# Weights' words by one shift-and-or and a bfloat16-to-float16 copy, in half pieces; split products for chunk 0's feed-forward; a new order

## The chip, the cores and the metric

The kernel runs on one NeuronCore of a Trainium2 chip, in one launch. The metric is the device time of one execution in microseconds (us), as the median of several runs. The engines are PE (matrix products), DVE (vector), ACT (scalar), POOL (GpSimd) and SP, which here only issues transfers.

## The reference

A recurrent attention and then a feed-forward part with a maximum of three products in place of an activation. The weights `moe_w1`, `moe_w2`, `moe_w3`, `moe_w_out` arrive as 64-bit floats, all else as 32-bit floats.

```python
B, H, S, D = 4, 8, 768, 48          # batch, heads, steps, head width
for t in range(S):
    cur = einsum('bhd,bhe->bhde', u * k[t], v[t])
    y[t] = einsum('bhd,bhde->bhe', r[t], state + cur)
    state = w * state + einsum('bhd,bhe->bhde', k[t], v[t])
x = y, as 3072 rows of 384
h = maximum(maximum(x @ w1, x @ w2), x @ w3)      # 384 -> 768
out = h @ w_out                                   # 768 -> 384
```

## The kernel before

The 768 steps are cut into 12 chunks of 64 steps (`NCH`, `C`). The heads of a chunk are worked on in two halves, q = 0 and 1, of 8 units each. With the powers of `w` multiplied into `k` and `r` (`scale`), the attention of a chunk is: scores on PE, a mask on DVE with the `u` term on its diagonal (`product`, `total`, `diagonal`, `mask`), values on PE (from the masked scores and from the state before the chunk), and keys on PE, which bring the state forward (`into_state`). The result, transposed, is `x`: 256 tokens a chunk. The feed-forward of a chunk is 18 up products (6 blocks f of 128 columns, three weights i each, three matmuls of 128 x 256 a product) and a down part of 3 banks by 6 blocks. ACT copies the first product of a block to `m` (`first`), DVE folds in the other two (`least`).

From chunk 1 on, every factor is split into a high and a low part, and a product is three matmuls: high by high, low by high, high by low. In attention the parts are float16; in the feed-forward they are the float32r format (`xh`, `xl` for x; `hh`, `hl` for h; `wh`, `woh` and a low tile, `wlo` in the profile, for the weights). The left factors of attention's matmuls stand in tiles with gaps, `kb` (scores), `vb` (values), `ktb` (keys), `sb` (state), which transfers on SP fill from dense tiles `kd`, `vd`, `ktd`, `sd` (`spread`); the right ones are `rh`, `rl`, `ah`, `al`. Chunk 0 is different: attention (`full`, with `apart` filling the tiles on ACT) and feed-forward (the `else` branch of `mul`, and `part`) are done in plain float32 on the weights' words (`words`), so that the low parts need not be there yet.

The weights are 8 pieces of 1152 numbers on each partition, 6 for the up products and 2 for the down part. A piece comes as 64-bit words (`load_weight`, tile `raw64`). `convert` makes 32-bit words of them with three DVE instructions, lines 224 to 226, with the sign turned over (hence `ALU.min` in `least`); `round_up`, line 230, makes the high part on ACT; `leave`, line 234, subtracts it on DVE, after all pieces have been converted. Late in the kernel every piece is loaded again (`again`) to check on DVE and ACT that its exponents lie in the range that the conversion takes; if not, or if other checks fail, a slow general version behind a branch runs.

POOL (`helper`, `helping`) does scaling, products, diagonals and decay from chunk 2 on, and `hl` for blocks 0 to 4; before that DVE does them. The banks of PSUM are two pools of four: `psm` for the feed-forward, `psa` for attention. An up product takes the next `psm` bank as soon as its last reader is done.

The order of the instructions on each engine is written out by `Plan`. Each step is given an engine, a cost, a due time in chunks, what it reads, writes and takes from pools; `order` then plays the program through, taking on the engine that can start earliest the step with the lowest due time. A table `SHIFT` moves due times by kind of step, in chunks, with one number for the opening (due up to 1.6) and one for the rest. An argument `near` makes DVE steps dearer while POOL is busy. Each engine runs its list strictly in that order, and so does SP's list of transfers:

```python
t = min(when.values())
n = min((m for m in when if when[m] <= t + 0.02), key=lambda m: self.todo[m]["due"])
```

## Time and profile before

| what | value |
|---|---|
| runs | 424.49, 423.60, 424.29 us; median 424.29 |
| the profiled execution | 423.27 us, of which its span, first to last instruction, 421.5 us |
| TensorE clock granted | 1.000 |
| PE busy | 400.4 us (95% of the span) |
| DVE, ACT, POOL busy | 299.0, 245.4, 202.9 us |

The profile is one execution. Its page gives busy time by engine, the span in 40 slices of busy tenths, the chain of work that ended last, and the costliest groups of instructions. A group's row reads: line, engine, operation, output <- inputs, shapes, count, busy time, mean ns of one, and idle time before it with what ended it. PEld is the loading of weights into the array, which overlaps with PE's products. Tile names are cut short, so `raw` is `raw64`.

### The profile page before, as it was taken

Reading aid. Unit: us, or ns where it says so; the run is one execution under the profiler, and the core shown is the slowest. Engines: PE = TensorE matmul, PEld = TensorE weight load, DVE = VectorE, ACT = ScalarE, POOL = GpSimd, SP = SyncE. Lnnn points to the kernel's source line nnn. Section 1 sums busy time; section 2 is a strip of 40 time slices with the busy share of each in tenths; the row PEclk is TensorE's granted clock in tenths of the full one; section 3 lists DMA queues with packets and bytes.
Section 4 is the critical chain, followed back from the end, with each engine's and each line's share of the span. In section 5 each row is a group of like instructions: output and inputs, shape, how many; then the busy total and the mean of one; then the engine's idle time right before and its main releaser. Section 6 shows DMA issues by size and latency. Waiting matters only on the chain.

```text
span 421.5 us, 11698 instructions
## 1 busy us (share of the span) xinstructions
PE 400.4 (95%) x4686; PEld 390.7 (93%) x4686; DVE 299.0 (71%) x522; ACT 245.4 (58%) x612; POOL 202.9 (48%) x188
## 2 busy tenths in 40 slices
PE   2899999878999999999999999999999999999995
PEld 2898888868989999999999999999999999999995
DVE  6999999999998666765765765665665686354240
ACT  5798527454566656465466466366365478578241
POOL 8000008799679556555565555655564471011120
PEclk9999999999999999999999999999999999999999
DMA  8799897848889886965965975975875997856101
GB/s 297 303 330 287 252 273 236 239 104 264 262 213 274 227 222 167 286 177 136 277 185 144 273 188 146 271 186 147 265 189 154 262 343 210 261 191 226 39 2 45
DMA packets 28654, 90.12 MB, mean 214 GB/s; under 512 B 4528, under 2 KB 9392, under 8 KB 26544
## 3 DMA queue, kind: packets, MB, share of 16 engines
q1 hardware_dynamic: 23264, 84.47, 69.0%
q10 hardware_dynamic: 5328, 4.82, 3.6%
q8 instruction: 39, 0.64, 0.7%
q14 instruction: 23, 0.19, 0.2%
HBM read 45.85 MB, written 4.72 MB: 120 GB/s over the span
## 4 chain that ended last, share of the span: by engine, by line
PE 71%; DVE 11%; DMA 5%; issue 4%; ACT 4%; POOL 4%; SPq 0%; ACTq 0%; DVEq 0%; POOLq 0%
PE psm L463 59%; PE psa L385 11%; DVE wlo L225 2%; DMA out_dram<-io 1%; DMA ktb<-ktd 1%; DVE wlo L224 1%; DMA sb<-sd 1%; POOL hl L484 1%; DVE wlo L226 1%; DMA feat<-in_feat_dram 1%; PE psa L458 1%; DVE m L478 1%; POOL am L362 1%; POOL feat L342 1%; DVE wlo L234 1%
## 5 line engine op out<-in xcount | busy, mean ns | idle before, releaser
L463 PE MATMUL psm<-xh,wh 128*128 128x256 f32 x594 | 152.4, 287 | 2.3 <-DVE m L478 2.3
L463 PE MATMUL psm<-xl,wh 128*128 128x256 f32 x594 | 149.6, 282 | 0.0
L463 PEld LDWEIGHTS psm<-xh,wh 128*128 128x128 f32 x594 | 112.3, 189 | 3.3 <-DVE m L478 3.2
L463 PEld LDWEIGHTS psm<-xl,wh 128*128 128x128 f32 x594 | 112.3, 189 | 0.6 <-DVE xl L446 0.5
L463 PE MATMUL psm<-xh,wlo 128*128 128x256 f32 x594 | 103.0, 282 | 0.0
L478 DVE TENSOR_TENSOR m<-psm,m 128x256 f32<-128x256 f32 x138 | 57.8, 419 | 60.4 <-PE psm L463 45.4
L463 PEld LDWEIGHTS psm<-xh,wlo 128*128 128x128 f32 x594 | 85.3, 192 | 0.0
L342 POOL TENSOR_TENSOR feat<-feat,wrt 128x512 f32<-128x512 f32 x40 | 56.7, 1428 | 59.3 <-DMA feat<-in_feat_dram 59.2
L484 POOL TENSOR_TENSOR hl<-m,hh 128x256 fp32r<-128x256 f32 x55 | 47.1, 855 | 78.0 <-ACT hh L481 77.9
L481 ACT CAST hh<-m 128x256 fp32r<-128x256 f32 x66 | 26.8, 407 | 73.2 <-DVE m L478 72.9
L361 POOL TENSOR_TENSOR am<-tok,u_sb 128x384 f32<-128x384 f32 x20 | 24.4, 1222 | 57.9 <-DVE al L405 57.9
L463 PE MATMUL psm<-hh,woh 128*128 128x256 f32 x198 | 50.2, 286 | 0.0
L463 PE MATMUL psm<-hh,wlo 128*128 128x256 f32 x198 | 49.3, 281 | 0.0
L325 ACT ACTIVATE junk<-tok 128x384 bf16<-128x384 f32 x72 | 37.5, 521 | 7.5 <-DMA tok<-in_tok_dram 5.9
L463 PEld LDWEIGHTS psm<-hh,woh 128*128 128x128 f32 x198 | 37.5, 189 | 0.0
L463 PEld LDWEIGHTS psm<-hh,wlo 128*128 128x128 f32 x198 | 37.5, 189 | 0.0
L441 ACT ACTIVATE xh<-psa 32x256 fp32r<-32x256 f32 (+5 forms) x60 | 25.0, 417 | 19.1 <-PE psa L385 18.4
L446 DVE SCALAR_TENSOR_TENSOR xl<-psa,xh 32x256 fp32r<-32x256 f32 (+2 forms) x55 | 25.9, 470 | 13.9 <-ACT xh L441 13.0
L463 PE MATMUL psm<-hl,woh 128*128 128x256 f32 x198 | 32.6, 281 | 1.8 <-POOL hl L484 1.8
L314 DVE TENSOR_TENSOR kd<-feat,kd 128x512 f16<-128x512 f32 x22 | 21.3, 970 | 17.4 <-ACT kd L309 17.3
L385 PE MATMUL psa<-ah,vb 128*128 128x64 f16 x352 | 32.8, 194 | 0.0
L385 PE MATMUL psa<-al,vb 128*128 128x64 f16 x176 | 31.2, 193 | 1.4 <-DVE al L405 1.4
(102 smaller groups left out, 819.8 us busy)
## 6 DMA issues: line engine op xcount, KB each, us to landing
tok<-in_tok_dram SPq DMA_DIRECT2D x24, 576.0 KB, 6.6
raw<-in_ws_dram SPq DMA_DIRECT2D x12, 1152.0 KB, 8.2
feat<-in_feat_dram SPq DMA_DIRECT2D x24, 512.0 KB, 5.3
kb<-kd SPq DMA_DIRECT2D x22, 256.0 KB, 5.3
kb<-kd SPq DMA_DIRECT2D x22, 248.0 KB, 5.6
ktb<-ktd SPq DMA_DIRECT2D x20, 256.0 KB, 3.6
ktb<-ktd SPq DMA_DIRECT2D x20, 248.0 KB, 4.8
raw<-in_wo_dram SPq DMA_DIRECT2D x4, 1152.0 KB, 6.3
```

The source lines that it names most:

```text
L225: nc.vector.scalar_tensor_tensor(out=t, in0=rw[:, :, 0], scalar=29, in1=t, op0=ALU.logical_shift_right, op1=ALU.bitwise_or)
L314: nc.vector.tensor_tensor(out=dense.dense[:, 1, :, 0:w], in0=src, in1=dense.dense[:, 0, :, 0:w], op=ALU.subtract)
L325: nc.scalar.activation(out=junk, in_=src, func=AF.Square, scale=scale, accum_out=stat[:, kind, 2 * c + q:2 * c + q + 1])
L342: helper(c).tensor_tensor(out=t[n], in0=t[n], in1=tb, op=ALU.mult)
L361: helper(c).tensor_tensor(out=w.rearrange("p (g b) d -> p g b d", g=2), in0=t["r"], in1=by_token(u_sb, q), op=ALU.mult)
L385: nc.tensor.matmul(out=ps, lhsT=l[i], rhs=rr[j], start=first and n == 0, stop=last and n == 2)
L441: nc.scalar.mul(out=hi, in_=src, mul=SC_X)
L446: nc.vector.scalar_tensor_tensor(out=lo, in0=src, scalar=SC_X, in1=hi.bitcast(F32), op0=ALU.mult, op1=ALU.subtract)
L463: nc.tensor.matmul(out=ps, lhsT=a, rhs=b, start=first and n == 0, stop=last and n == len(prods) - 1)
L478: nc.vector.tensor_tensor(out=to, in0=ps, in1=m, op=ALU.min)
L481: nc.scalar.copy(out=h[0][:, f, :], in_=m)
L484: (nc.vector if f == NF - 1 else nc.gpsimd).tensor_tensor(out=h[1][:, f, :], in0=m, in1=h[0][:, f, :].bitcast(F32), op=ALU.subtract)
```

## The change

A weight's piece is loaded as two halves of 576 numbers (`HN`), as 16-bit words, at an offset of one 16-bit word in the tile, so that bits 16 to 47 of each number lie on a 32-bit word (`mids`). `tops`, on ACT, copies the top 16 bits of each number, read as bfloat16, into the upper halves of the words of a zeroed tile `ztop`, as float16; that turns the 11-bit exponent into an 8-bit one. `convert` is now one DVE instruction for a half, in place: shift the middle word right by 13, or the `ztop` word in. `round_up` and `leave` then work on each half at once, from `mids`. The sign is no longer turned, so `least` takes the maximum. The low parts have tiles of their own, `wl0` to `wl7`. `raw64` has four half buffers for two whole ones. The vetting works on halves of 32-bit words and a different test.

Chunk 0's feed-forward now uses the split products like the others, so chunk 0's x and h get low parts (`leave_x`; all of chunk 0's `hl` on DVE). `full` for the keys takes 112 of 128 columns. Chunk 2's scaling, products and decay move from POOL to DVE, its diagonals to ACT. The opening's column of `SHIFT`, the `near` rule and several costs are new; the other column is the same but for new and dropped kinds.

```diff
-        "act ah": (-2.85, -0.9), "act am": (-0.15, 0), "act hh": (-0.7, 0.4), ...
+        "act ah": (-5.31, -0.9), "act am": (2.08, 0), "act hh": (1.37, 0.4), ...
...
-                cost += self.NEAR * p["near"] * min(cost, free["pool"] - t)
+                cost += min(p["near"] * cost, p["near"] / (1 + p["near"]) * (free["pool"] - t))
...
-    wld = ctx.enter_context(tc.tile_pool(name="wld", bufs=2))
+    wld = ctx.enter_context(tc.tile_pool(name="wld", bufs=4))
...
-    wlo = ctx.enter_context(tc.tile_pool(name="wlo", bufs=NF + 3))
...
-    def convert(n, raw64, his):
-        rw = raw64.rearrange("p (n two) -> p n two", two=2)
-        t = wlo.tile([P, WN], I32, name="wlo")
-        words[n] = t.bitcast(F32)
-        nc.vector.tensor_scalar(out=t, in0=rw[:, :, 1], scalar1=0x0F000000, scalar2=3, op0=ALU.bitwise_xor, op1=ALU.logical_shift_left)
-        nc.vector.scalar_tensor_tensor(out=t, in0=rw[:, :, 0], scalar=29, in1=t, op0=ALU.logical_shift_right, op1=ALU.bitwise_or)
-        nc.vector.scalar_tensor_tensor(out=t, in0=rw[:, :, 1], scalar=-2 ** 27, in1=t, op0=ALU.bitwise_and, op1=ALU.bitwise_xor)
-        return his
-    def round_up(n, his):
-        nc.scalar.copy(out=his, in_=words[n])
-    def leave(n, his):
-        lows[n] = wlo.tile([P, WN], F32R, name="wlo")
-        nc.vector.tensor_tensor(out=lows[n], in0=words.pop(n), in1=his.bitcast(F32), op=ALU.subtract)
...
-        nc.scalar.activation(out=left, in_=left, func=AF.Abs, accum_out=odd[:, n:n + 1])
+    lows = [const.tile([P, WN], F32R, name=f"wl{n}") for n in range(NW)]
...
+    def load_weight(n, h, shift=0):
+        raw = wld.tile([P, 4 * HN + 4], I16, name="raw64")
+        src = (ws[n] if n < NF else wo[n - NF]).bitcast(I16)
+        nc.sync.dma_start(out=raw[:, shift:shift + 4 * HN], in_=src[:, h * 4 * HN:(h + 1) * 4 * HN])
+        return raw
+    ztop = [const.tile([P, HN], I32, name=f"ztop{h}") for h in range(2)]
+    for z in ztop:
+        nc.gpsimd.memset(z.bitcast(F32), 0.0)
+    def halves(raw, k):
+        return raw[:, 0:4 * HN].rearrange("p (n four) -> p n four", four=4)[:, :, k]
+    def mids(raw):
+        return raw.bitcast(I32)[:, 1:1 + 2 * HN].rearrange("p (n two) -> p n two", two=2)[:, :, 0]
+    def tops(h, raw):
+        nc.scalar.copy(out=ztop[h].bitcast(F16).rearrange("p (n two) -> p n two", two=2)[:, :, 1], in_=halves(raw[:, 1:], 3).bitcast(BF16))
+    def convert(h, raw):
+        nc.vector.scalar_tensor_tensor(out=mids(raw), in0=mids(raw), scalar=13, in1=ztop[h], op0=ALU.logical_shift_right, op1=ALU.bitwise_or)
+    def round_up(n, h, raw):
+        nc.scalar.copy(out=part_of(n, h)[0], in_=mids(raw).bitcast(F32))
+    def leave(n, h, raw):
+        hi, lo = part_of(n, h)
+        nc.vector.tensor_tensor(out=lo, in0=mids(raw).bitcast(F32), in1=hi.bitcast(F32), op=ALU.subtract)
...
+        nc.scalar.activation(out=t.bitcast(F32), in_=t, func=AF.Relu, bias=beyond, accum_out=odd[:, k:k + 1])
...
-        return nc.gpsimd if c > 1 else nc.vector
+        return nc.gpsimd if c > 2 else nc.vector
...
-        if c == 1:
+        if c in (1, 2):
...
-        nc.vector.tensor_tensor(out=to, in0=ps, in1=m, op=ALU.min)
+        nc.vector.tensor_tensor(out=to, in0=ps, in1=m, op=ALU.max)
...
+    def lows_by(c, f):
+        return nc.gpsimd if f < NF - 1 and c > 0 else nc.vector
...
+        dma(due, fetch, 8 * P * HN, takes=[("raw64", w)])
+        do(due - 0.05, "act", act(HN), lambda: tops(h, T[w]), reads=[w], writes=[("ztop", h)])
+        do(due, "dve", dve(HN), lambda: convert(h, T[w]), reads=[("ztop", h)], writes=[w], near=0.55)
+        do(due + 0.05, "act", act(HN), lambda: round_up(n, h, T[w]), reads=[w], writes=[("his", n, h)])
+        do(due + 0.1, "dve", dve(HN), lambda: leave(n, h, T[w]), reads=[w, ("his", n, h)], writes=[("lo", n, h)], near=0.6)
...
-        do(due, "pe", 3.65, lambda: full("ke", q, ktb, D, P, units(raws[c, q]["v"])), reads=["ktb", t], takes=[("psa", ("ke", c, q))])
+        do(due, "pe", 3.2, lambda: full("ke", q, ktb, D, C + D, units(raws[c, q]["v"])), reads=["ktb", t], takes=[("psa", ("ke", c, q))])
...
-                        for j in range(NJ):
-                            nc.tensor.matmul(out=ps, lhsT=by_up(words[f], i, j), rhs=T["x", 0][:, j, :], start=j == 0, stop=j == NJ - 1)
+                    T["up", c, f, i] = up(T["x", c], f, i, TOK)
```

How the order moves, engine by engine. First ACT, the last twelve rows up to its first copy of an up product to `m` (`junk` are sums of squares for the checks, `am` the diagonals, `sd` the state's high part). Before:

```order
L452 ACTIVATE ktb<-tok 64x8x48 x2
L325 ACTIVATE junk,stat<-tok 128x384
L373 ACTIVATE am<-cs,a 128x64 x8
L309 ACTIVATE kd<-feat 128x8x64
L441 ACTIVATE xh<-psa 96x256
L441 ACTIVATE xh<-psa 32x256 x3
L419 ACTIVATE state<-psa 128x192 x2
L325 ACTIVATE junk,stat<-tok 128x384
L230 CAST wh<-wlo 128x1152
L325 ACTIVATE junk,stat<-tok 128x384
L347 CAST rh<-feat 128x512
L474 COPY m<-psm 128x256
```

The same twelve rows up to that copy now; line 239 is `tops`, line 246 `round_up`:

```order
L239 CAST ztop_109<-raw_293 128x576
L349 ACTIVATE junk,stat<-tok 128x384 x3
L332 ACTIVATE vd_147<-tok 128x8x48
L239 CAST ztop_110<-raw_311 128x576
L443 ACTIVATE state<-psa 112x192 x2
L246 CAST wh<-raw_273 128x576
L349 ACTIVATE junk,stat<-state 128x384
L332 ACTIVATE kd<-feat 128x8x64
L246 CAST wh<-raw_293 128x576
L332 ACTIVATE sd<-state 128x8x48
L246 CAST wh<-raw_311 128x576
L498 COPY m<-psm 128x256 x2
```

The copy stood behind the third weight's rounding; now it stands behind four weights' tops and roundings, chunk 1's second diagonals not included, and behind both halves' state and `sd`.

Second DVE, from the second decay of chunk 0 on: the first weight (`raw_165`), before:

```order
L381 TENSOR_TENSOR tok<-tok,tkt 128x384
L224 TENSOR_SCALAR wlo<-raw_165 128x1152
L225 SCALAR_TENSOR_TENSOR wlo<-raw_165,wlo 128x1152
L226 SCALAR_TENSOR_TENSOR wlo<-raw_165,wlo 128x1152
L224 TENSOR_SCALAR wlo<-raw_167 128x1152
L225 SCALAR_TENSOR_TENSOR wlo<-raw_167,wlo 128x1152
L226 SCALAR_TENSOR_TENSOR wlo<-raw_167,wlo 128x1152
```

The same place now; line 243 is the shift-and-or, line 250 the subtraction, `raw_177` and `raw_179` the first weight's halves:

```order
L243 SCALAR_TENSOR_TENSOR raw_177<-raw_177,ztop_109 128x576
L405 TENSOR_TENSOR tok<-tok,tkt 128x384
L243 SCALAR_TENSOR_TENSOR raw_179<-raw_179,ztop_110 128x576
L250 TENSOR_TENSOR wl_101<-raw_177,wh 128x576
L470 SCALAR_TENSOR_TENSOR xl<-psa,xh 96x512
L250 TENSOR_TENSOR wl_101<-raw_179,wh 128x576
L243 SCALAR_TENSOR_TENSOR raw_181<-raw_181,ztop_109 128x576
```

The subtractions, which came after the last weight, follow each half, and chunk 0's `xl` stands among them.

Third PE, where chunk 0's feed-forward begins. Before:

```order
L458 MATMUL psa<-feat,kb 128x64 x8
L458 MATMUL psa<-tok,ktb 128x48 x8
L458 MATMUL psa<-am,vb_126 96x64 x8
L458 MATMUL psa<-tok,ktb 128x48 x8
L823 MATMUL psm<-xh,wlo 128x256 x27
```

Now:

```order
L482 MATMUL psa<-feat,kb 128x64 x8
L482 MATMUL psa<-tok,ktb 112x48 x8
L482 MATMUL psa<-am,vb_139 96x64 x8
L487 MATMUL psm<-xh,wh 128x256
L487 MATMUL psm<-xl,wh 128x256
L487 MATMUL psm<-xh,wh 128x256
L487 MATMUL psm<-xl,wh 128x256
L487 MATMUL psm<-xh,wh 128x256
L487 MATMUL psm<-xl,wh 128x256
L487 MATMUL psm<-xh,wl_101 128x256 x3
L482 MATMUL psa<-tok,ktb 112x48 x8
```

The second batch of keys moves behind the first up product, and that product needs `xl` and the first weight's low half. Further on, 8 up products of chunk 1 stand ahead of chunk 0's down part, which before was finished first.

More of the change, by code (lines that the diff above doesn't have):

```diff
@@ L80, in do @@
         need.discard(n)
-        self.todo.append(dict(n=n, due=due, eng=eng, cost=cost, fn=fn, need=need, takes=takes, size=size, near=near, kind=kind, touch={*reads, *writes, *new}))
+        self.todo.append(dict(n=n, due=due, eng=eng, cost=cost, fn=fn, need=need, takes=takes, size=size, near=near, kind=kind, late=late, touch={*reads, *writes, *new}))
     def order(self, free):
@@ L636, in general @@
                     put(m, leaving(banks[m], P))
-    plan = Plan(dict(feat=2, tok=3, raw64=2, wlo=NF + 3, psa=4, psm=4, rh=2, rl=2, am=2, a=2, ah=1, al=1, xh=2, xl=2, m=3, io=3, hh=1, hl=1))
+    plan = Plan(dict(feat=2, tok=3, raw64=4, psa=4, psm=4, rh=2, rl=2, am=2, a=2, ah=1, al=1, xh=2, xl=2, m=3, io=3, hh=1, hl=1))
     do = plan.do
@@ L704, in before_mask @@
         h, cost = helping(c, U * D)
-        do(due - 0.16, h, 2 * cost, lambda: product(c, q), reads=[t], takes=[("am", ("am", c, q))], writes=[("kdec", c, q)], near=1)
+        do(due - 0.16, h, 2 * cost, lambda: product(c, q), reads=[t], takes=[("am", ("am", c, q))], writes=[("kdec", c, q)], near=0.55)
         do(due - 0.08, "dve", dve(U * D), lambda: total(c, q), reads=[("am", c, q)], takes=[("a", ("a", c, q))])
-        h, cost = helping(c, U * C) if c != 1 else ("act", U * 0.2)
-        do(due - 0.05, h, cost, lambda: diagonal(c, q), reads=[("a", c, q)], writes=[("am", c, q)], near=1)
+        h, cost = helping(c, U * C) if c not in (1, 2) else ("act", 2.0)
+        do(due - 0.05, h, cost, lambda: diagonal(c, q), reads=[("a", c, q)], writes=[("am", c, q)], near=0.55)
         squares(c, q, due - 0.15)
@@ L713, in before_keys @@
         h, cost = helping(c, U * D)
-        do(due - 0.30, h, cost, lambda: decay(c, q), reads=[t, "tkt"], writes=[("kdec", c, q)], near=1)
+        do(due - 0.30, h, cost, lambda: decay(c, q), reads=[t, "tkt"], writes=[("kdec", c, q)], near=0.55)
         do(due - 0.24, "act", act(U * D), lambda: high(ktd, units(raws[c, q]["k"]), D), reads=[t, ("kdec", c, q)], writes=["ktdh"])
-        do(due - 0.23, "dve", dve(U * D), lambda: low(ktd, units(raws[c, q]["k"]), D), reads=[t, ("kdec", c, q), "ktdh"], writes=["ktdl"], near=1)
+        do(due - 0.23, "dve", dve(U * D), lambda: low(ktd, units(raws[c, q]["k"]), D), reads=[t, ("kdec", c, q), "ktdh"], writes=["ktdl"], near=1.2)
         dma(due - 0.20, lambda: spread(nc.sync, ktb, ktd, C), 524288, reads=["ktdh", "ktdl"], writes=["ktb"], n=2)
@@ L781, in valued, with leave_x @@
     def valued(c, q, due):
+        do(due, "pe", 1.42, lambda: values(c, q), reads=[("vb", q), ("sb", q), ("ah", c, q), ("al", c, q), ("rh", c, q), ("rl", c, q)], takes=[("psa", ("va", c, q))])
+        leave_x(c, q, due)
+    def leave_x(c, q, due):
         def x_hi():
@@ L790, in x_lo @@
             x_low(c, q, *T["x", c])
-        do(due, "pe", 1.42, lambda: values(c, q), reads=[("vb", q), ("sb", q), ("ah", c, q), ("al", c, q), ("rh", c, q), ("rl", c, q)], takes=[("psa", ("va", c, q))])
         hi, lo = ("xh", c), ("xl", c)
@@ L894 @@
     for n in range(NW):
-        weight(n, 0.11 * n - 0.4)
+        for h in range(2):
+            weight(n, h, 0.11 * n + 0.05 * h - 0.4)
     for q in range(2):
@@ L907 @@
     for n in range(NW):
-        again(n, NCH - 2.6 + 0.25 * n)
-    do(2.9, "dve", 0.5, check_ends, reads=[("begun", 2)], writes=["ends"])
+        for h in range(2):
+            again(n, h, NCH - 2.6 + 0.25 * n + 0.12 * h)
+    do(4.9, "dve", 1.2, check_ends, reads=[("begun", 4)], writes=["ends"])
     do(NCH - 0.4, "dve", 1.5, check, reads=["ends", "odd", *(k for k in plan.wrote if k[0] == "sq")], writes=["good"])
```

195 lines of the change are left out of this document (80 added, 115 removed), and 10 rows, old and new, of the table SHIFT.

## The prediction

> **What bounds the kernel now.** I read the page's head and its 40 slices first, to see which engine is full and where that changes. Each slice is 10.5 us.
>
> ```profile
> span 421.5 us, 11698 instructions
> PE 400.4 (95%) x4686; PEld 390.7 (93%) x4686; DVE 299.0 (71%) x522; ACT 245.4 (58%) x612; POOL 202.9 (48%) x188
> ...
> PE   2899999878999999999999999999999999999995
> ...
> DVE  6999999999998666765765765665665686354240
> ACT  5798527454566656465466466366365478578241
> POOL 8000008799679556555565555655564471011120
> PEclk9999999999999999999999999999999999999999
> ```
>
> PE is full, at full clock, except in the first slice, slices 7 to 9 and the last. DVE is full from slice 1 to 12 and has room afterwards. So there is an opening of about 125 us that DVE takes part in, and a long rest that is PE alone. The stretches below are cut at the points where the chunks change on PE; columns are length, then busy time of PE, PEld, DVE, ACT and POOL.
>
> ```profile
> 0.00:29.30 29.30, 20.39 (x100) 19.68 (x101) 25.04 (x46) 20.26 (x48) 8.70 (x15) 1.00 0.86 314
> 29.30:68.38 39.08, 38.74 (x338) 33.85 (x338) 37.56 (x54) 23.47 (x59) 3.71 (x2) 1.00 0.96 282
> 68.38:107.70 39.32, 33.07 (x388) 31.38 (x387) 39.18 (x50) 22.03 (x61) 36.95 (x26) 1.00 0.69 190
> 107.70:125.00 17.30, 16.39 (x236) 15.74 (x235) 17.00 (x30) 10.08 (x29) 11.98 (x13) 1.00 0.87 254
> 125.00:390.00 265.00, 265.00 (x3415) 263.62 (x3411) 172.26 (x319) 160.89 (x400) 137.84 (x130) 1.00 0.76 216
> ```
>
> First stretch: attention of chunk 0, PE idle 8.9 us. Second: chunk 0's feed-forward with chunk 1's attention, PE idle 0.3 us. Third: chunk 1's feed-forward with chunk 2's attention: PE idle 6.3 us, DVE busy 39.18 of 39.32. The fourth loses 0.9 us, the fifth nothing. So whatever the change wins or loses shows in the time at which PE finishes chunk 1's feed-forward, 107.7 before (the cut of the third stretch); what follows is a block of PE work that moves with it. PE's waits of the third stretch, from the list of waits, end on DVE or on POOL; the three longest of its matmuls:
>
> ```profile
> PE psa L385 <- DVE rl L352: 1.6, 1, 1.6
> PE psa L385 <- DVE al L405: 1.4, 1, 1.4
> PE psm L463 <- POOL hl L484: 1.8, 1, 1.8
> ```
>
> **PE's own work.** The first two rows are chunk 0's plain float32 products (two matmul records for each), the third a run of split products in the chain, then a piece of chunk 1's attention in the chain, and two of the opening's batches of eight:
>
> ```profile
> 29.30 13.59 PE L823 MATMUL psm<-xh,wlo 128*128 128x256 f32 x54
> 43.42 5.43 PE L823 MATMUL psm<-xh,wlo 128*128 128x256 f32 x24
> ...
> 384.43 20.32 PE psm L463 x171
> ...
> 132.93 2.12 PE psa L385 x72
> ...
> 23.33 2.79 PE L458 MATMUL psa<-am,vb 128*96 128x64 f32 x16
> 25.91 3.59 PE L458 MATMUL psa<-tok,ktb 128*128 128x48 f32 x16
> ```
>
> A plain product is 2 x 5.43 / 24 = 0.45 us where nothing delays it; a split one is three of 20.32 / 171 = 0.119, or 0.357. For 54 up and 18 down products that is 72 x 0.095 = 6.9 us less (8.6 against the first run's slower pace, if that lasted). The keys' batch takes 112 columns for 128: at the pace between 2.79 for 96 and 3.59 for 128 it is 3.2, twice 0.4 saved. But PE had next to no idle time in the second stretch and will have some now: the split products need low halves of weights and of x that the plain ones did not, and ACT and DVE must make them first. So these 7.7 us count only as far as those two keep up.
>
> **ACT gates the start.** ACT's pieces, from its groups by shape and from its timeline:
>
> ```profile
> L230 ACT CAST wh<-wlo 128x1152 fp32r<-128x1152 f32 x6 | 6.9, 1150 | 6.4 <-DVE wlo L226 6.4
> L243 ACT ACTIVATE raw<-raw 128x1152 f16<-128x1152 f16 x8 | 22.8, 2855 | 3.1 <-DVE raw L239 2.6 <-DVE rl L352 0.5
> L325 ACT ACTIVATE junk<-tok 128x384 bf16<-128x384 f32 x72 | 37.5, 521 | 7.5 <-DMA tok<-in_tok_dram 5.9 <-ACT io L507 0.8
> ...
> 14.09 1.04 ACT L452 ACTIVATE vb<-tok 64x384 f32<-64x384 f32 x2
> 15.14 1.27 ACT L452 ACTIVATE kb<-feat 64x512 f32<-64x512 f32 x2
> ...
> 23.04 0.61 ACT L347 CAST rh<-feat 128x512 f16<-128x512 f32 x1
> ...
> 25.58 2.00 ACT L373 ACTIVATE am<-cs,a 128x64 f32<-128x64 f32 x8
> 27.49 0.61 ACT L309 ACTIVATE kd<-feat 128x512 f16<-128x512 f32 x1
> 28.01 1.54 ACT L441 ACTIVATE xh<-psa 96x256 f32<-96x256 f32 x4
> ...
> 32.58 0.38 ACT L474 COPY m<-psm 128x256 f32<-128x256 f32 x1
> ```
>
> In the order of after, ACT has `vb` of the second half done at 14.1 (15.13 before, less the `ktb` pair, about 1.05, that now comes later). Between that and the first `m` copy of chunk 0 stand: 8 `tops`, 8 half roundings, the `kb` pair (1.27), two `ktb` pairs (2.1), eight square sums, 0.52 each and a short read of the accumulator (4.8), eight diagonals (1.9), four `xh` pieces (1.55) and one of 0.5, two `kd` and one `rh` at 0.52 from start to start (1.6), and two each of `sd`, `vd` and the state's pairs, which I estimate at 0.43 by the same pace (2.6). Without the 16 new pieces that is 16.3 us. A half rounding is (1.150 - 0.19) / 2 + 0.19 = 0.67, or 0.58 from start to start, 4.6 for eight; 0.19 is my estimate of the fixed part, from `rh`'s 0.61 for 512 columns and the 1.15 for 1152.
>
> The `tops` copy is the change's unknown: it reads 2-byte elements 8 bytes apart and writes 2-byte elements 4 bytes apart, and no row shows that. Low end: the cast row, 0.67. High end: L243, the one ACT row with 2-byte elements spread out, 2.855 for 1152, which scales to 1.52. I take 0.67, because every cast to a second buffer that the trace has, `rh` to 2 bytes included, runs at one pace, while L243 also works in place and accumulates; but spacing and element size speak for L243, so the high end keeps a large chance. With 0.67 the eight cost 4.6, the sum is 25.5 and the first copy cannot start before 39.6; with the short waits for DVE between, I take 41.5. It was 32.6.
>
> The Trainium skill (ScalarE: Activation LUTs, section "What ACT_TABLE_LOAD costs") gives every ACTIVATE 186 ns and 0.833 ns for an element, for fp32 and bf16 alike: L230 agrees (1.15), L243 does not (2.855 where the rule has 1.15). By the rule `tops` is 0.67 and the time is my forecast; by L243 it is the first rival below.
>
> That copy matters because PE has four `psm` banks: after four up products it must wait for the first copy. By 41.5 PE can have done the opening, four up products, the second `ktb` batch and one batch of scores. What is left to the end of chunk 1's feed-forward is 57.0 us: 14 and 18 up products of nine matmuls (34.2), both chunks' 54 down matmuls (12.9), and 336 matmuls of attention at 2.12 / 72 = 0.0294 (9.9).
>
> `tops` and the half rounding also put two new waits into ACT's line: `tops` for the shift-and-or that last read its `ztop` buffer, two halves earlier, and the rounding for its own half's shift-and-or. All of ACT's work stands behind them, the `xh` pieces, copies and diagonals among it, and PE and DVE wait for those. DVE's shift follows each `tops` within a row or two, so I price these waits at the 1.9 us by which 41.5 lies above 39.6; their low end is nothing.
>
> **DVE sets the pace after it.** DVE's rows; where three numbers stand behind the colon they are the shortest, the median and the longest, in ns:
>
> ```profile
> L224 DVE TENSOR_SCALAR wlo<-raw x8: 747/752/754, 15.0 to 60.3; 128x1152 int32<-128x1152 int32 x8
> L225 DVE SCALAR_TENSOR_TENSOR wlo<-raw,wlo 128x1152 int32<-128x1152 int32 x8 | 10.9, 1359 | 0.3
> L234 DVE TENSOR_TENSOR wlo<-wlo,wh x6: 1344/1739/2307, 64.2 to 85.8; 128x1152 fp32r<-128x1152 f32 x6
> L239 DVE TENSOR_SCALAR raw<-raw x8: 749/753/1492, 343.5 to 399.9; 128x1152 int32<-128x1152 int32 x8
> L478 DVE TENSOR_TENSOR m<-psm,m 128x256 f32<-128x256 f32 x138 | 57.8, 419 | 60.4 <-PE psm L463 45.4 <-ACT m L474 10.2 <-ACT ktd L309 1.4
> L484 DVE TENSOR_TENSOR hl<-m,hh 128x256 fp32r<-128x256 f32 x11 | 5.4, 486 | 4.2 <-ACT hh L481 4.2
> L446 DVE SCALAR_TENSOR_TENSOR xl<-psa,xh 96x512 fp32r<-96x512 f32 x11 | 7.5, 684 | 12.3 <-ACT xh L441 12.3
> L342 DVE TENSOR_TENSOR feat<-feat,wrt 128x512 f32<-128x512 f32 x8 | 5.3, 684 | 0.5 <-DMA feat<-in_feat_dram 0.5
> ```
>
> A weight cost DVE 0.75 + 1.36 + 1.36 and later 1.74, together 5.2; now two halves of 0.68 + 0.67, or 2.7. In place at 8 bytes costs DVE nothing (L239 at 0.749 against L224 at 0.747). Eight weights: 20 us less. Added: x's low half for chunk 0 (2.4), its six `hl` (2.9), and chunk 2's scaling, products and decay that POOL did (4 x 0.68, and 6 narrower ones that I put at 0.53: 5.9). Net 9 us less. From the first copy to weight 7's second low half DVE has 16 maxima (0.4 each where POOL is idle, 6.5), 8 shift-and-ors and 8 subtractions (10.8), six `hl` (2.9), `xl` (2.4) and nine pieces of attention of 0.5 to 0.75 (about 5.9): 28.5 us. With the copy's 0.4 and 1 us of waiting weight 7 is ready at 71.4. PE meanwhile runs ahead with 8 products of chunk 1, and its own remaining work is 28.4 us: chunk 0's down part (6.4), ten up products (10.7), 168 matmuls of attention (4.9), chunk 1's down part (6.4). There ACT has square sums, `hh` and diagonals queued ahead of copies that PE's banks wait for, and DVE prepares chunk 2: I allow 3.5 us, nearly half of the 6.3 that the third stretch loses now, since the 1.74 us subtractions are gone from it. Sum: 71.4 + 28.4 + 3.5 = 103.3, against 107.7: 4.4 us less.
>
> **Edits with one answer.** Transfers: a whole piece lands 8.2 us after its issue (row below); the first halves, issued right behind the first inputs as before, at 3.5 us, are there before ACT's 14.1. Half pieces put eight more issues on SP for the weights and eight for the vetting, each behind the release of one of four buffers; what stands behind them on SP are the spreads of `kb`, `sb`, `vb` and `ktb`, and by the sums above each release comes before those are due. The 2-byte shift of the destination costs between nothing and a doubled landing, again about 8 us for a half; a buffer released by its subtraction is used 9 us or more later, which covers it, and without that cover each late half would cost its lateness on ACT.
>
> ```profile
> raw<-in_ws_dram SPq DMA_DIRECT2D x12, 1152.0 KB, 8.2
> ```
>
>  The new POOL memsets run before 12 us, when POOL has nothing else to do. Vetting moves 32-bit words in the last third, where PE waits for nobody. The tail behind PE's last matmul is not touched.
>
> The profiled execution took 423.27 (span 421.5 and 1.8 around it), 1.0 under the median of 424.29. 423.3 - 4.4 = 418.9; as a median, 420.
>
> **Rivals.** (1) `tops` costs 1.52, as L243 scales. Then the eight ahead of the first copy add 6.8 us, and the eight behind it another 6.8, of which ACT's slack there (about 24 us of work in 29.5) takes 5: chunk 1 ends some 8.5 us later, 424.3 - 4.4 + 8.5 = 428.5, slower. It decides from 8 x d = 4.4, d = 0.55, so from a `tops` of about 1.2. For it: the only spread 2-byte row. Against it: in place and accumulating, that row is not this operation. (2) DVE and ACT keep up and PE has no gap after 41.5: 41.5 + 57.0 = 98.5, 9.2 us less, 415. For it: DVE's 9 us and POOL's chunk 2 work gone; against it: DVE is full until 71 by my sum. (3) ACT's roundings too slow down, reading 4-byte words 8 bytes apart: another 13 us, above 436. Nothing but L243 speaks for it. (4) The waits only change places, as ACT's start 9 us later takes all that PE and DVE win: 424, no change.
>
> **Numbers.** My forecast 0.40, (1) 0.33, (2) 0.12, (3) 0.07, (4) 0.08. The range 414 to 431 holds forecast, (1), (2) and (4); the forecast's own is 417 to 423. Under 0.2% (0.85 us) a measurement of this kernel cannot tell a change from none: faster 0.51, same 0.09, slower 0.40.
>
> **What would show it.** `tops` near 0.67 or near 1.5 decides first. Then chunk 0's first `m` copy near 41, PE idle between the fourth up product and it, the last subtraction of a weight near 71, and the end of chunk 1's feed-forward near 103, with about 314 us behind it as before. The prediction is wrong if a weight's half lands after ACT is ready for it, if PE waits in the fifth stretch, or if ACT, not DVE, is full between 41 and 71.

## The result, and the profile after

The changed kernel takes 417.03 us (median of 4 runs, 416.47 to 418.29) where the kernel before takes 424.26: a ratio of 0.984, interval 0.981 to 0.986, so 7.2 us less. The forecast was 420 as a median and 4.4 us less on the profiled runs; the profiled run of the changed kernel, 418.29 (span 416.4), is the slowest of its four and 5.0 below the profiled 423.27 of before.

The page of the changed kernel, its first line, the busy times and PE's row of 40 slices:

```profile
span 416.4 us, 11971 instructions
PE 392.5 (94%) x4758; PEld 387.9 (93%) x4758; DVE 282.5 (68%) x551; ACT 256.7 (62%) x674; POOL 183.3 (44%) x180
PE   2869899999899999999999999999999999999995
```

PE has 7.9 us less to do than before (400.4). The 8 at the eleventh digit (104 to 115 us) is a gap that the forecast did not have. The gain is told by one pair of windows: from the start to the end of chunk 1's feed-forward, first of before, then of the changed kernel.

```profile
0.00:107.60 107.60, 92.11 (x821) 84.80 (x822) 101.69 (x148) 65.66 (x166) 49.26 (x42) 1.00 0.84 257
```

```profile
0.00:100.90 100.90, 85.49 (x893) 83.33 (x894) 89.47 (x170) 83.89 (x209) 28.43 (x35) 1.00 0.90 270
```

Columns: stretch, its length, then busy time of PE, PEld, DVE, ACT and POOL, PE's granted clock, the transfers' share, GB/s. PE works 6.6 us less (92.11 to 85.49) and idles as long as before: 15.5 and 15.4. DVE has 12 us less, ACT 18 more. The idle time has only moved, as the same columns by stage show:

```profile
20.00:43.00 23.00, 17.17 (x110) 16.36 (x111) 20.53 (x36) 21.82 (x56) 0.00 (x0) 1.00 0.93 263
43.00:60.00 17.00, 17.00 (x253) 16.87 (x253) 16.28 (x34) 14.71 (x35) 0.00 (x0) 1.00 0.97 279
43.00:100.90 57.90, 57.09 (x733) 56.65 (x733) 54.04 (x102) 47.29 (x123) 17.99 (x16) 1.00 0.91 262
101.00:125.00 24.00, 20.37 (x277) 19.76 (x276) 16.67 (x31) 14.07 (x39) 13.78 (x13) 1.00 0.87 229
```

From 20 to 43 PE idles 5.8 us and ACT is nearly full (21.82 of 23.00); from 43 to 100.9 PE idles 0.8 us, where the third stretch of before lost 6.3. Behind 101 it loses 3.6 us in this run. The new pieces, by their line (shortest, median and longest, in ns):

```profile
L239 ACT CAST ztop<-raw x16: 819/842/879, 14.2 to 66.7; 128x576 f16<-128x576 bf16 x16
L246 ACT CAST wh<-raw x12: 692/717/733, 16.9 to 56.2; 128x576 fp32r<-128x576 f32 x12
L243 DVE SCALAR_TENSOR_TENSOR raw<-raw,ztop x16: 743/756/761, 15.1 to 67.7; 128x576 int32<-128x576 int32 x16
```

L239 is `tops`, L246 the half rounding, L243 the shift-and-or. Where ACT has no wait, the piece behind a `tops` starts 0.71 us after it (at 16.15 and 16.86, for one pair), so that is what it takes of ACT's line. The steps that the prediction named, from the timelines of ACT, DVE and PE (start, duration, line, operation, and in brackets the wait ahead of it):

```profile
42.30 0.64 ACT L498 COPY m<-psm 128x256 f32<-128x256 f32 x2
42.72 0.38 PE L487 MATMUL psm<-xh,wh 128*128 128x256 f32 x1 [1.32 <-ACT m L498]
69.46 0.75 DVE L250 TENSOR_TENSOR wl<-raw,woh 128x576 fp32r<-128x576 f32 x1
100.85 0.28 PE L487 MATMUL psm<-xh,wh 128*128 128x256 f32 x1
```

The last row is chunk 2's first up product. In before it stood at 107.57:

```profile
107.57 0.28 PE L463 MATMUL psm<-xh,wh 128*128 128x256 f32 x1
```

That is 6.7 us earlier, with 315.5 us of span behind it where before had 313.9. The 1.6 us given back lie mostly in the eleventh slice. ACT's transfers of chunk 1's output (L873) stand at the head of its queue there, and the copies of `io` behind them:

```profile
102.88 0.34 ACTq L873 DMA_DIRECT2D out_dram<-io  x1
103.26 0.37 ACT L534 COPY io<-psm 128x256 f32<-128x256 f32 x1 [2.82 <-DMA kb<-kd]
```

The first operand was ready at 100.4 (its copy of `io` began at 100.06), yet the transfer was issued at 102.9, and the wait ended with another transfer's landing; the second waited as long, and PE then 2.0 us for a copy of `io` to free a bank.

### The profile page after: what moved, and what is told of

Same layout as the page of the kernel before. It is cut to its first block, busy times and chain, and to the rows that moved or that the text cites. A ratio compares the mean times of both kernels' runs of the same rounds, so it can differ in the third digit from the quotient of the medians.

```text
span 416.4 us, 11971 instructions
## 1 busy us (share of the span) xinstructions
PE 392.5 (94%) x4758; PEld 387.9 (93%) x4758; DVE 282.5 (68%) x551; ACT 256.7 (62%) x674; POOL 183.3 (44%) x180
## 4 chain that ended last, share of the span: by engine, by line
PE 80%; ACT 9%; DVE 4%; DMA 3%; issue 2%; POOL 1%; ACTq 0%; DVEq 0%; POOLq 0%
PE psm L487 67%; PE psa L409 12%; DMA tok<-in_tok_dram 3%; ACT junk L349 2%; ACT ztop L239 1%; ACT wh L246 1%; ACT kb L476 1%; DVE kd L337 1%; ACT kd L332 0%; ACT ktb L476 0%; DMA wu_sb<-in_wu_dram 0%; ACT xh L465 0%; ACT am L397 0%; DVE al L429 0%; POOL am L385 0%
## 5 line engine op out<-in xcount | busy, mean ns | idle before, releaser
L487 PE MATMUL psm<-xh,wh 128*128 128x256 f32 x648 | 166.3, 286 | 6.2 <-ACT xh L465 2.9
L487 PE MATMUL psm<-xl,wh 128*128 128x256 f32 x648 | 163.4, 282 | 1.1 <-DVE xl L470 1.1
L487 PEld LDWEIGHTS psm<-xh,wh 128*128 128x128 f32 x648 | 123.3, 190 | 6.7 <-ACT xh L465 3.1
L487 PE MATMUL psm<-xh,wl 128*128 128x256 f32 x648 | 112.6, 283 | 0.0
L487 PEld LDWEIGHTS psm<-xh,wl 128*128 128x128 f32 x648 | 92.7, 190 | 0.0
L487 PE MATMUL psm<-hh,wl 128*128 128x256 f32 x216 | 53.4, 279 | 0.0
L487 PEld LDWEIGHTS psm<-hh,wl 128*128 128x128 f32 x216 | 40.6, 188 | 0.0
L470 DVE SCALAR_TENSOR_TENSOR xl<-psa,xh 32x256 fp32r<-32x256 f32 (+2 forms) x60 | 28.3, 471 | 13.9 <-ACT xh L465 12.9
L465 ACT ACTIVATE xh<-psa 32x256 fp32r<-32x256 f32 (+2 forms) x60 | 25.0, 417 | 17.0 <-PE psa L409 16.0
L409 PE MATMUL psa<-rh,sb 128*128 128x64 f16 x352 | 32.5, 193 | 0.0
L498 ACT COPY m<-psm 128x256 f32<-128x256 f32 x72 | 26.3, 367 | 9.5 <-PE psm L487 8.1
```

Of the source, the lines that this page charges most:

```text
L409: nc.tensor.matmul(out=ps, lhsT=l[i], rhs=rr[j], start=first and n == 0, stop=last and n == 2)
L465: nc.scalar.mul(out=hi, in_=src, mul=SC_X)
L470: nc.vector.scalar_tensor_tensor(out=lo, in0=src, scalar=SC_X, in1=hi.bitcast(F32), op0=ALU.mult, op1=ALU.subtract)
L487: nc.tensor.matmul(out=ps, lhsT=a, rhs=b, start=first and n == 0, stop=last and n == len(prods) - 1)
L498: nc.scalar.copy(out=m, in_=ps)
```

## The experiments

Theory: PE's end of chunk 1's feed-forward carries the time, ACT's line of work up to the first copy of `m` gates PE's start into chunk 0's feed-forward, and DVE paces from there to 70. Rivals: ACT only fills time that others set; PE's own work, not DVE's, sets the pace behind 43; the gain is the order's or one part's alone; the loss behind 101 is not the output transfers'.

**The changed kernel again.**

> The changed kernel once more, unaltered, so that the next three are set against it on the same chip: 416.4 to 418.3 us, as its four runs so far.

416.39 us (415.30 to 417.34), ratio 0.982 [0.980, 0.984]. The profiled run, 415.30 (span 413.5), has chunk 2's first product at 100.86, as before it within 0.01, and behind it:

```profile
100.90:125.00 24.10, 23.32 (x304) 22.95 (x304) 17.74 (x33) 16.23 (x46) 16.26 (x16) 1.00 0.94 252
```

Here the second copy of `io` came at 101.16, where the first profile had it at 103.26, PE idled 0.8 us where the first profile had 3.6, and the span is 2.9 shorter. So the opening repeats to a hundredth of a us, and what differs between these two runs is the stretch behind it. The kernel and its queues are the same in both, so the loss of the first profile is not in every execution.

**Tops twice.** Every copy of tops issued a second time, with the same result.

```diff
+        nc.scalar.copy(out=ztop[h]..., in_=halves(raw[:, 1:], 3).bitcast(BF16))
         nc.scalar.copy(out=ztop[h]..., in_=halves(raw[:, 1:], 3).bitcast(BF16))
```

> Each copy of the tops is issued twice, so 16 more copies stand on ACT, 8 of them ahead of the first copy of m at 42.3 us; the records are 0.84 us each, but start 0.70 apart. Theory of the prediction (ACT's run of work up to the first copy of m is the gate): that copy moves to 46 to 48, chunk 1's end by 4 to 6 and the time to 421 to 423. Rival (the transfers and DVE set the pace, and ACT's work only fills what it waits anyway): 417 to 418.

429.29 us (428.98 to 430.38), ratio 1.012 [1.010, 1.014]: 12.9 more than the repeat above, twice the theory's upper end. Its copy of `m`, PE's product behind it, PE's end of chunk 1, and three windows:

```profile
49.27 0.65 ACT L499 COPY m<-psm 128x256 f32<-128x256 f32 x2
49.70 0.38 PE L488 MATMUL psm<-xh,wh 128*128 128x256 f32 x1 [3.15 <-ACT m L499]
116.08 0.28 PE L488 MATMUL psm<-xh,wh 128*128 128x256 f32 x1
```

```profile
0.00:116.10 116.10, 90.03 (x893) 86.64 (x894) 91.31 (x170) 97.14 (x226) 28.79 (x35) 0.97 0.78 241
52.00:54.00 2.00, 2.00 (x11) 2.00 (x11) 1.40 (x3) 2.00 (x7) 0.00 (x0) 0.50 0.96 284
98.60:102.00 3.40, 3.40 (x31) 3.40 (x28) 2.46 (x5) 3.34 (x14) 3.32 (x5) 0.50 0.71 182
```

The copy moved by 7.0, and that is what the eight pieces ahead of it cost: the second of a pair writes the tile of the first and starts 0.85 to 0.88 us behind it (at 43.80 and 44.68, for one pair), not 0.71, and the eight distances add up to 6.9. Chunk 1's end moved by 15.2: PE idles 10.4 us more than in the repeat (26.1 for 15.7), and its busy time grew by 4.8 on the same matmuls, part of it in two spells under a granted clock of 0.50, one behind the wait for `m` and one from 98.6 to 102. ACT is the gate, and the prediction's first rival (a `tops` of 1.52 gives 428.5) was a real danger: here the longer run of `tops` cost 12.9 us in all for 7.0 up to the copy.

**PE kept busy.** Five matmuls of constants ahead of the first up product, whose results are overwritten.

```diff
+        for k in range(5):
+            nc.tensor.matmul(out=ps, lhsT=ident, rhs=cs[:, 0:n], start=True, stop=True)
```

> Five matmuls of constants, 256 columns each, are added on PE straight ahead of the first up product, in time in which PE stands idle (26.3 to 30.9 us in the changed kernel's trace); nothing else differs. In that trace the first split products start 0.21 us apart from 30.9 to 38.8, and 0.118 apart from 39.0 on. Theory A (PE is slow only because it had been idle, and gets up to speed by being busy, sooner if it is kept busy sooner): the pace of 0.118 begins 2 to 5 us earlier, and since PE waits for ACT's m copy at 42.7 already, at most 2 us arrive at the end: 415 to 416.5. Theory B (the slow pace is set by something outside PE, its operands or the transfers of that time): nothing moves, 416.4 to 418.3.

417.92 us (417.38 to 419.67), ratio 0.985 [0.983, 0.987]: 1.5 more than the repeat. The time lies in theory B's range, but not for B's reason, as things did move. PE in this run, ahead of its wait and behind it, with a window of its clock:

```profile
34.70 0.28 PE L489 MATMUL psm<-xl,wh 128*128 128x256 f32 x1
34.82 0.28 PE L489 MATMUL psm<-xh,wh 128*128 128x256 f32 x1
...
42.72 0.58 PE L489 MATMUL psm<-xh,wh 128*128 128x256 f32 x1 [4.07 <-ACT m L504]
43.09 0.41 PE L489 MATMUL psm<-xl,wh 128*128 128x256 f32 x1
43.31 0.41 PE L489 MATMUL psm<-xh,wh 128*128 128x256 f32 x1
```

```profile
46.00:48.00 2.00, 2.00 (x12) 2.00 (x11) 1.04 (x4) 1.17 (x3) 0.00 (x0) 0.52 0.90 270
```

Theory A's first half came: the pace of 0.118 us began at 34.7 instead of 39.0, so PE's slowness is its own. But the copy of `m` is at 42.3 as ever, so PE idled 4.07 us for it, and the products behind the wait started 0.21 apart with half the clock granted; chunk 1's end is at 105.83, 5.0 later in this run. PE got faster where it was not the gate, and paid for the idle time behind it.

**Chunk 1's output from SP's queue.**

```diff
-lambda: nc.scalar.dma_start(out=out[m, :, c * TOK:(c + 1) * TOK], ...
+lambda: (nc.sync if c == 1 else nc.scalar).dma_start(out=out[m, :, c * TOK:(c + 1) * TOK], ...
```

> Chunk 1's three output transfers are issued from SP's queue instead of ACT's; nothing else differs. In the changed kernel's trace two of them sat at the head of ACT's queue for 2.82 and 2.81 us (100.4 to 102.9 and 103.6 to 106.1), with the copies of io behind them, and PE then waited 2.0 us for a copy of io (108.0). Theory A (the 1.6 us given back between chunk 1's end and 119 us are this wait): ACT's two waits go, PE's 2.0 us shrinks to under 0.5, and the time falls by 1.5 to 2.5 to about 415. Theory B (PE's waits there come from the state's transfers of chunk 2, late for themselves): ACT's waits go but PE's idle time shows elsewhere before 120 us, and the time stays within 0.7 of 417.

414.95 us (414.10 to 417.01), ratio 0.979 [0.976, 0.981]: 1.4 below the repeat of the unaltered kernel, with ranges that overlap, and the lowest median of all. ACT's copies of `io`, and the stretch behind them:

```profile
100.01 0.65 ACT L534 COPY io<-psm 128x256 f32<-128x256 f32 x2
101.73 0.35 ACT L534 COPY io<-psm 128x256 f32<-128x256 f32 x1
```

```profile
101.00:125.00 24.00, 23.71 (x315) 23.36 (x314) 18.05 (x35) 16.67 (x46) 18.13 (x18) 1.00 1.01 269
```

All three copies are done by 102.1 (107.96 in the first profile), PE idles 0.3 us, and 311.8 us stand behind chunk 1's end for 315.5. That fits theory A: the wait of the first profile stood in ACT's queue, and with the transfers on SP it is gone. It is not shown that moving them is what took it away. The repeat, with the transfers on ACT, lost only 0.8 us there, and among the kernels below one with the transfers on ACT has 311.7 us behind chunk 1's end, where the issues waited for nothing but the copies of `io` just ahead of them (0.41 us). So an issue from ACT can be held, by 2.8 us in the first profile, and often is not. That the move is worth 1.4 us in the median is not shown either.

**Tops on POOL.**

```diff
-        nc.scalar.copy(out=ztop[h]..., in_=halves(raw[:, 1:], 3).bitcast(BF16))
+        nc.gpsimd.tensor_copy(out=ztop[h]..., in_=halves(raw[:, 1:], 3).bitcast(BF16))
```

> The 16 copies of the tops go to POOL, which is idle from 29 to 68 us; nothing else differs from the changed kernel. ACT loses 8 copies, 0.70 us apart, ahead of the first copy of m at 42.3. Theory A (ACT's run of work up to that copy is the gate, as the 7.0 us it moved when the copies were doubled says): the copy of m moves to 37 to 39, DVE (36.4 of 39.1 us busy from 29.3 to 68.4) lets 1.5 to 3 of it through, and the time is 413.5 to 415.5. Rival 1 (a copy on POOL takes over 2 us and each weight's shift-and-or waits for it): first copy of m at 43 or later, 418 to 425. Rival 2 (POOL's copies make DVE's pieces longer by 10% and more while both run): 416 to 419 with the m copy earlier.

415.90 us (415.02 to 417.21), ratio 0.982 [0.978, 0.985], as the changed kernel. The time lies just above theory A's range, though its copy of `m` is where A had it. That copy, chunk 1's end and POOL's pieces:

```profile
38.72 0.36 ACT L498 COPY m<-psm 128x256 f32<-128x256 f32 x1
99.90 0.28 PE L487 MATMUL psm<-xh,wh 128*128 128x256 f32 x1
L239 POOL CAST ztop<-raw x16: 831/1131/3084, 11.4 to 62.8; 128x576 f16<-128x576 bf16 x16
```

The gate opened 3.6 us sooner, and 0.95 arrived at chunk 1's end. PE was not there to use the rest: its products still started 0.21 us apart up to 39.4, so the second copy of `m` waited 1.03 us for PE, and behind 43 PE idled 1.5 us (of 56.9) for 0.8. The pieces of DVE's shift-and-or were 0.83 us on the mean for 0.76, one of 1.33 among them, which is the second rival in a small way.

**Both, busy PE and tops on POOL.**

> The tops on POOL and the five constant matmuls ahead of PE's first up product, together. With the matmuls alone PE's pace of 0.118 us began at 34.7 instead of 39.0, PE then stood idle 4.07 us for the first copy of m, and after that ran at 0.212 again up to 48.5, with a granted clock of 0.50 from 42 to 48. Theory A (what costs is PE's idle time of 4 us, which the tops on POOL shorten to under 2): the slow pace does not come back, and this one is 0.5 to 2 us below the kernel with the tops on POOL alone. Rival (the pace drops whatever PE waits): the slow pace comes back near 43, and the time is 0 to 2 above that kernel's.

418.19 us (413.95 to 420.11), ratio 0.988 [0.984, 0.991]. In the profiled run, the fastest (413.95), the copy of `m` is at 38.35, PE's wait for it 2.4 us, the granted clock stays at 1.00 and chunk 1's end is at 100.52, with 311.7 us behind it (the output transfers are on ACT here). That PE keeps its pace behind 2.4 us is theory A, that it is worth time is not: the other three runs are 418.1 and more, and the medians say 2.3 slower than the tops alone. There is a profile of the fastest run only, so where the others lost it stays open.

**One part alone: the words.** The kernel before with the new conversion on whole pieces.

```diff
-        nc.vector.tensor_scalar(out=t, in0=rw[:, :, 1], scalar1=0x0F000000, scalar2=3, ...
-        nc.vector.scalar_tensor_tensor(out=t, in0=rw[:, :, 0], scalar=29, in1=t, ...
-        nc.vector.scalar_tensor_tensor(out=t, in0=rw[:, :, 1], scalar=-2 ** 27, in1=t, ...
+        nc.vector.scalar_tensor_tensor(out=t, in0=mids, scalar=13, in1=ztop, ...
...
+        do(due - 0.05, "act", 1.5, lambda: tops(*T["raw", n]), reads=[("raw", n)], writes=["ztop"])
```

> The kernel before with one part of the change: a weight's words are made by the copy of tops (ACT, one of 1152 elements), one shift-and-or (DVE) and the shifted load, on whole pieces; chunk 0's feed-forward is still in plain float32 products, and the order comes from the numbers of before with the new costs. Theory A (DVE bounds before from 60 to 107.6, 47.3 of 47.6 us busy, and PE idles 6.6 us there): with 16 us less on DVE most of PE's 6.6 goes: 418 to 421. Theory B (it is the split products that won): 423 to 425. Rival (ACT, with 11 us more, becomes the bound): over 426.

426.26 us (424.92 to 429.20), ratio 1.006 [1.004, 1.009]: slower by 2.0, against theory A. The time lies at the lower end of the third rival's range, but not for its reason: ACT is nowhere full.

```profile
43.00:60.00 17.00, 16.77 (x140) 14.79 (x139) 10.05 (x17) 12.37 (x21) 0.00 (x0) 1.00 0.92 231
60.00:80.00 20.00, 9.24 (x125) 7.79 (x123) 16.46 (x17) 10.17 (x23) 5.37 (x4) 0.93 0.72 199
80.00:107.60 27.60, 18.68 (x203) 18.30 (x204) 23.13 (x33) 12.66 (x37) 24.60 (x20) 0.74 0.78 212
```

DVE did get its time, but from 43 to 60 (10.05 of 17 busy), where PE was full with plain products; the subtractions still stood behind the last word, and PE idles 19.7 us from 60 to 107.6. Of these 11.75 come at once, up to 85.17, ahead of scores whose `rl` DVE finished at 85.0, behind seven subtractions; in that wait the granted clock fell to 0.50. DVE's time was freed where nobody waited for it. This is so in the order that the old numbers give; the words alone in an order made for them were not tried.

**The other part alone: split products in chunk 0.** The kernel before, the old conversion, a tile of its own for each low half.

```diff
-        lows[n] = wlo.tile([P, WN], F32R, name="wlo")
+    lows = [const.tile([P, WN], F32R, name=f"wl{n}") for n in range(NW)]
...
-                    if c:
-                        T["up", c, f, i] = up(T["x", c], f, i, TOK)
-                    else: ...
+                    T["up", c, f, i] = up(T["x", c], f, i, TOK)
...
-        low_weight(n, 0.8 + 0.11 * n)
+        low_weight(n, 0.11 * n - 0.3)
```

> The kernel before with the other part: chunk 0's feed-forward in split products, with the old conversion in three DVE operations on whole pieces, and the weights' lows in tiles of their own; the order again from the numbers of before. Theory A (the parts need each other: PE's saving of 6.9 us only turns into waits for DVE, which has to make words and lows, 4.75 us a weight, ahead of chunk 0): 424 to 430. Theory B (PE's saving carries by itself): 416 to 420.

445.71 us (444.15 to 447.26), ratio 1.051 [1.046, 1.055]. Theory A's side, far beyond its range:

```profile
45.73 0.58 PE L463 MATMUL psm<-xl,wh 128*128 128x256 f32 x1 [15.72 <-DVE xl L446]
20.00:43.00 23.00, 9.17 (x46) 8.68 (x45) 22.72 (x26) 15.95 (x42) 0.00 (x0) 1.00 0.84 283
```

`xl`, a new step in chunk 0, stood on DVE's list behind three words and two subtractions of 1152, DVE is full (22.72 of 23.00), and PE waits 15.7 us at once. How much of it a better order would take away was not tried; that PE's saving does not come without DVE's relief is shown for this order only.

**The old order.** The changed kernel with the numbers of `SHIFT` of before, as far as it has them.

```diff
-        "act ah": (-5.31, -0.9), "act am": (2.08, 0), "act hh": (1.37, 0.4), ...
+        "act ah": (-2.85, -0.9), "act am": (-0.15, 0), "act hh": (-0.7, 0.4), ...
```

> The changed kernel with the numbers that set the order of before wherever both have one (new kinds of work keep the new numbers): the words, the half pieces and chunk 0's split products are those of the changed kernel, only the order differs. Theory A (the new operations carry the gain and the order only fits them): 417 to 421. Theory B (without the new order the gain is not there, as the two kernels with one part each and the old numbers took 426.3 and 445.7): 424 to 440.

427.38 us (424.95 to 428.82), ratio 1.009 [1.007, 1.011]: theory B, 10 us above the changed kernel, with chunk 1's end at 108.42.

```profile
60.00:64.00 4.00, 1.69 (x47) 1.48 (x46) 3.48 (x7) 3.03 (x6) 0.00 (x0) 1.00 1.02 322
64.00:68.00 4.00, 1.86 (x7) 1.57 (x8) 3.19 (x7) 3.25 (x7) 0.00 (x0) 0.63 1.02 274
```

PE has the same work and idles 5.3 us in the stretch from 43 to 101 (0.8 with the new order), 4.5 of it in these eight us, with a drop of the clock behind it. So the gain needs an order that fits the new operations. What the new order would do for the old operations was not tried.

**Output on SP, residues on POOL; then tops on POOL too.** The five residues of chunk 0 that DVE made go to POOL; the second kernel has the tops there as well.

```diff
-        lows_by(c, f).tensor_tensor(out=h[1][:, f, :], ...
+        (nc.gpsimd if f < NF - 1 else nc.vector).tensor_tensor(out=h[1][:, f, :], ...
```

> The kernel with chunk 1's output transfers on SP's queue, and chunk 0's residues of the squares (hl, five of the six) on POOL instead of DVE: 5 pieces of 0.41 us leave DVE between 48 and 66 us, where it was 16.3 of 17.0 and 9.8 of 10.0 us busy; POOL, idle there, takes 0.74 for such a piece. Theory A (DVE paces from 43 to 70): the last subtraction of a weight starts at 67.5 to 68.5 instead of 69.5, and 0.5 to 1.5 us of it reach the end: 413.5 to 414.5. Rival (DVE only fills its queue there, and chunk 1 waits for PE's own work): 414.5 to 415.5. Rival 2 (a later hl holds chunk 0's down products): 416 and more.

> As the kernel with the output transfers on SP's queue and the residues on POOL, and the 16 copies of tops on POOL as well (1.13 us each there by the run that moved them alone, which took 415.9, no gain that its interval tells). Theory A (with both ACT and DVE relieved the opening gets shorter by what each gave, 0.7 us of the last subtraction from the tops and 1 to 2 from the residues): 412.5 to 414. Rival (POOL's queue is in order, so residues wait behind tops that wait for a load, and the opening gets no shorter): 414.5 to 418.

416.38 us (413.80 to 418.23), ratio 0.982 [0.979, 0.985], and 415.21 (414.44 to 417.18), ratio 0.980 [0.978, 0.982]: neither beats the transfers on SP alone. Of the first its last subtraction and a window; chunk 1's end is at 100.85 in the first and at 100.95 in the second:

```profile
69.45 0.75 DVE L250 TENSOR_TENSOR wl<-raw,woh 128x576 fp32r<-128x576 f32 x1
43.00:60.00 17.00, 17.00 (x253) 16.86 (x252) 15.41 (x30) 14.74 (x35) 3.79 (x5) 1.00 0.97 281
```

With 0.9 us less on DVE (16.28 to 15.41) the last subtraction moved by 0.01 and chunk 1's end by nothing, and PE is still full (17.00 of 17.00): theory A falls. In the second kernel ACT is far from full (39.5 us busy of 57.9) and PE idles 3.1 us in place of 0.8, and the end stays too.

**What in the layout costs.** The changed kernel, and behind its last work copies of 576 elements on ACT, one of a kind to a line; twice around, of which these are the second round, back to back; the first has the same durations.

```diff
+    nc.scalar.copy(out=hd, in_=d1)    # packed to packed, L921
+    nc.scalar.copy(out=hd, in_=b1)    # read at 8 bytes, L922
+    nc.scalar.copy(out=h4, in_=d1)    # written at 4 bytes, L923
+    nc.scalar.copy(out=h4, in_=b1)    # both, as tops, L924
+    nc.scalar.copy(out=h8, in_=d1)    # written at 8 bytes, L925
...
+    nc.scalar.copy(out=f2, in_=f1)    # 4-byte elements, read and written at 8 bytes, L929
+    nc.scalar.copy(out=h8, in_=h8)    # 2-byte elements at 8 bytes in place, L930
```

> The changed kernel, and behind its last work 2 x 10 copies on ACT of 576 elements in each of 128 partitions, which feed nothing, to see which part of the layout costs time; the time as a whole is of no use. In the traces so far such a copy took 0.67 to 0.72 us between packed elements, the copy of tops (2-byte elements, read every 8th and written every 4th byte) 0.84, and the sum over a weight (2-byte elements at every 8th byte, read and written in place, with an accumulation) 2.86 for 1152. Theory A (writing, or reading, 2-byte elements apart costs): one of the forms with 8-byte steps takes over 0.8 and the packed ones 0.6 to 0.7. Theory B (the layout costs nothing): all forms within 0.05 of each other.

```profile
420.73 0.67 ACT L921 CAST raw<-raw 128x576 f16<-128x576 bf16 x1
421.44 0.69 ACT L922 CAST raw<-raw 128x576 f16<-128x576 bf16 x1
422.16 0.83 ACT L923 CAST raw<-raw 128x576 f16<-128x576 bf16 x1
423.03 0.83 ACT L924 CAST raw<-raw 128x576 f16<-128x576 bf16 x1
423.89 1.47 ACT L925 CAST raw<-raw 128x576 f16<-128x576 bf16 x1
...
428.36 0.70 ACT L929 COPY raw<-raw 128x576 f32<-128x576 f32 x1
429.09 1.47 ACT L930 COPY raw<-raw 128x576 f16<-128x576 f16 x1
```

Theory A, and it is the writing: 2-byte elements written 8 bytes apart take 1.47, 4 bytes apart 0.83, packed 0.67; reading them apart costs 0.02, and 4-byte elements written 8 bytes apart 0.70. In place makes no difference (L925 and L930).

## Why the prediction came out as it did

- **PE's own work**, -7.7: right in the main. It is 6.6 us less up to chunk 1's end, with the first split products at the slow pace of 0.21 us up to 38.8; 85.49 and 15.41 of idle time make up 100.9. The aside of 8.6 does not come out of its row: 27 products in 13.59 us are 0.503 each, 0.146 above 0.357, or 10.5 for 72.
- **`tops`**, 0.67 between ends 0.67 and 1.52: the record lasts 0.84, a quarter above. In ACT's line it costs 0.71, where the sum has 4.6 / 8 = 0.58: 1.0 us more for eight, and the first copy of `m` came at 42.3 for 41.5. The high end was L243's, and the last experiment shows why it did not hold: L243's price is that of 2-byte writes at 8 bytes (1.47 here, 1.52 scaled); `tops` writes at 4. The rule that the prediction weighed (the Trainium skill, ScalarE: Activation LUTs, "What ACT_TABLE_LOAD costs": 186 ns + 0.833 ns an element for an ACTIVATE with immediate scale and bias) gives 0.67 for 576 elements, and L921 agrees (0.67). The copies written apart do not (0.83 and 1.47).
- **ACT gates the start**: shown, by the copy at 49.3 with doubled tops and at 38.7 with none on ACT. The break-even, 0.55 us more for a `tops`, holds: 0.87 more cost 12.9 us, so by proportion I estimate 0.54 for the 8.0 us between the medians 424.37 and 416.39.
- **DVE sets the pace behind it** is the step that failed. The last subtraction was ready at 70.2 for the 71.4 of the sum, which is near, but nobody waited for it:

```profile
42.72:70.20 27.48, 27.48 (x357) 27.30 (x358) 26.60 (x56) 22.94 (x50) 0.00 (x0) 1.00 0.96 295
70.20:100.85 30.65, 29.84 (x378) 29.57 (x377) 27.67 (x49) 24.61 (x74) 17.94 (x16) 1.00 0.87 234
```

  PE is busy without a gap up to that subtraction, and taking 0.9 us off DVE changed nothing. What stood in its place is the prediction's second rival in all but its price: 57.3 us of PE work behind the copy (57.0 in the sum) with 0.8 us of idle time, from 42.7 to 100.85. In the terms of the sum, 71.4 + 28.4 + 3.5, the three measure 70.2, 29.8 and 0.8: the 3.5 us allowed for ACT's copies and DVE behind 71 were 2.7 too many, PE had 1.4 more left to do, and the start was 1.2 earlier, so that 103.3 came out 2.4 too late.
- **The total is near in part by luck.** The profiled run, 418.29, is 0.6 below the forecast's 418.9 because two errors partly cancel: chunk 1's end 2.4 us earlier than forecast, and 1.5 us more behind it than the 314. The 7.2 us between the medians lie above the 5.0 between the profiled runs, as the profiled run of before is 1.0 below its median and that of the changed kernel 1.3 above; 417.0 is at the lower edge of the forecast's own 417 to 423.
- **314 us behind it**: 315.5 in one run, 312.6 in the repeat, 311.8 with the output on SP, 311.7 with busy PE and tops on POOL. "PE waits in the fifth stretch" was named as what would make the prediction wrong, and there PE idled 0.13 us; the loss came just ahead of it, in the fourth, where the prediction had left the 0.9 of before as it was. It had priced eight more issues on SP and not the transfers that ACT issues.
- **The half pieces** landed in time: up to 70 us no wait of ACT or DVE ends on a weight's load. The row is `x24`, 7.3 us where a whole one took 8.2.

```profile
raw<-in_ws_dram SPq DMA_DIRECT2D x24, 576.0 KB, 7.3
```

- **No part alone** did it in the old order: the words alone 426.3, the splits alone 445.7, both 427.4. The prediction's sums follow the new order and do not price it by itself; one part alone in the new order stays untested.
